# Retention attention and a feed-forward block on one core: v scaled for the states on GpSimd alone, late steps reordered

## The chip, the cores and the metric

One Trainium2 chip, one core of it. The metric is the device time of one execution in microseconds. Before the change three runs gave 206.89, 207.63 and 212.83 us, median 207.63. One execution was profiled: its own time is 207.04 us, the span from its first to its last instruction 205.2 us.

## What is computed

The reference, cut to its core. Batch 4, 8 heads, 768 positions, head width 64; then a feed-forward block with 512 and 2048 columns:

```python
gamma = 1.0 - 2.0 ** (-5.0 - np.arange(H))
for t in range(S):
    state = gamma * state + einsum('bhd,bhe->bhde', k[:, :, t], v[:, :, t])
    y[:, :, t] = scale * einsum('bhd,bhde->bhe', q[:, :, t], state)
x = y.transpose(0, 2, 1, 3).reshape(B, S, H * D)
xn = (x - mean) / np.sqrt(var + 1e-06) * g_ln
out = x + np.maximum(xn @ w_ch1, 0.0) @ w_ch2
```

All arrays come in and go out as float32; the kernel works in bfloat16 with float32 in PSUM.

## The kernel before

**Tiles.** The 4 x 768 positions are cut into 24 tiles of 128 positions: tiles 0 to 3 are the first chunk of each batch element, and tiles 4 to 23 are the later chunks, five per element. Up to tile 7 each tile has its own visit; from tile 8 on they come in pairs, (8, 9) to (22, 23).

**One tile's way.** `k`, `q`, `v` load a tile by DMA from GpSimd's queue (L361), and `gk`, `gq`, `gv` are gates behind them: a copy of one element out of the tile just loaded, on GpSimd (L390), which holds that queue until the load has landed. `tr` transposes q and k of a tile by DMA on SyncE's queue (L404). `eq` scales q (L410, VectorE). `vis` makes the scores of a pair on PE into the PSUM banks X0 to X3 (L419) and adds q times the state into Y0 and Y1 (L425). `am` multiplies the scores by the decay mask (L432, VectorE), `py` multiplies them with v (L447, PE). `bn`, `sr`, `rt` and `nb` make mean, 1/deviation and shift (L455, L586, L595, L590), `xc` copies y to SBUF (L471, ScalarE), `xg` normalizes it (L599, ScalarE), `ex` transposes that by DMA (L524).

**The state.** It is kept by chunks. `vg` makes v times the decay of each position and head (L478 on ScalarE, L481 on GpSimd), `pd` multiplies it with k and adds it up in the PSUM bank PD (L489), `pb` scales that into the bfloat16 `state` (L500 on ScalarE, L504 on VectorE). There are three buffers each for `vg` and `state`. The `vg` step in both forms:

```python
if eng == "A":
    for h in range(H):
        nc.scalar.activation(out=slot(vgs, chunk(t))[:, h, :], in_=v_of(t)[:, h, :],
                             func=AF.Copy, scale=vsc[:, c, h:h + 1])
    return
nc.gpsimd.tensor_tensor(
    out=slot(vgs, chunk(t)), in0=v_of(t),
    in1=vsc[:, c, :].unsqueeze(2).to_broadcast([P, H, D]), op=ALU.mult)
```

On ScalarE it is eight instructions, one for a head; on GpSimd it is one.

**The feed-forward block.** Tiles are put in 14 groups: eight of one tile, four of two, two of four. `m` is a first product into an X bank (L549), `r` its ReLU out of the bank into `h` (L560 on ScalarE, L562 on VectorE). For the first eight tiles `z` is the second product (L567) and `ad` adds x (L575); for these tiles the gain is in the normalized input, and `wg0` to `wg3` later multiply it into the four column blocks of the first weights (L607 on ScalarE, L609 on VectorE). The later tiles use Strassen's scheme with seven products: `s` is one product of the second multiplication (L736), `sa` the differences it needs (L725, VectorE), `o` the additions into the output tile `osb` (L750, VectorE), `tm` and `wm` the weight combinations (L619, L630). The last two groups use it for the first multiplication too: `f` products (L670), `fs` copies out of PSUM (L684, ScalarE), `fo` additions (L697, VectorE), `fq` and `fr` ReLUs (L702; L711 on ScalarE or L709 on VectorE). `st` stores a tile from ScalarE's queue.

**The order.** `ORDER`, lines 30 to 100, is a list of 1043 tokens written out. A loop at the end of the kernel emits each in turn, so each engine gets its instructions in the list's order and runs them in that order. A token's parts are the step, its tile or group, the engine after the first slash (A ScalarE, D VectorE, S SyncE's queue, nothing for the step's usual one), and the PSUM banks after the second. `vg10/A` is the state's v of tile 10 on ScalarE, `vg20/` that of tile 20 on GpSimd.

Of the kernel before, what the change touches and what calls it, by code (L numbers as in the profile page):

```python
# [52 lines left out]
am11a ad5 py10 r6_4/A py11 v14 pd11 m7_4//X1 bn11 pb12/A gq14 gk13 z6_0//M wg3/D st1/A gk15 r7_4/A
v13 pd12 bn10 m8_14//X0 sr11 xc11a q15 xc10b rt11 m8_8//X1 pb13 xc11b xc10a v15 sr10 nb11 z6_1 rt10
xg11b nb10 rs6 eq12 xg10b r8_14/A gk14 tr14 z6_2 wg1/D r8_8/A z6_3 v16 xg10a eq13 xg11a ex11/S
vis12//X0,X1,X2,X3 ad6 pd2 gv14 am13b vg14/ z7_0//M ex10/S pb14/A am12a m8_12//X3 gv13 am13a gq15
tr15 m8_2//X0 am12b tm4 py13 r8_2/A py12 z7_1 xc13a k16 xc13b bn12 r8_12/A pd14 m8_0//X0 vg15/A q16
bn13 z7_2 k17 sr13 m8_6//X1 xc12a rt13 q17 eq14 sr12 sq7 nb13 z7_3 rt12 pb15 xg13a v17 xg13b xc12b
m8_10//X2 ex13/S rs7 nb12 r8_6/A ad7 gv16 vg16/ r8_0/A m8_4//X1 r8_10/A gv15 xg12b k18 tm3 m9_8//X0
xg12a r8_4/A ex12/S pd15 st2/A eq15 s8_1//M r9_8/A sa8_1 st7/A gk17 vis14//X0,X1,X2,X3 pb16/A sa8_2  # L60
s8_5 gq17 am14a tr16 am14b pd16 gv17 m9_0//X0 gk16 am15a py14 am15b m9_4//X1 gk18 q20 py15 st3/A
m9_2//X2 tr17 bn15 r9_0/A k20 r9_4/A m9_6//X3 sa8_4 vg3/A q18 m10_2//X0 bn14 r9_6/A m9_12//X1 sa8_3
r9_2/A q19 sr14 s8_2//X3 sr15 r10_2/A o8_1 k19 xc15b vg17/A rt14 rt15 s8_6 nb15 pb17 gq20 s8_3 o8_2
r9_12/A eq16 xg15a m9_10//X0 xg15b o8_3 xc15a eq17 xc14b gq18 tr18 m9_14//X1 xc14a o8_4 v19 r9_10/A
nb14 wm3 xg14b s8_7 xg14a gq16 r9_14/A pd17 o8_5 vis16//X0,X1,X2,X3 pb18/A sa10_1 v18 tr19 s8_4
am16b gk19 am16a pd3 m10_4//X1 v20 ex15/S am17a py16 gq19 o8_6 st5/A m10_6//X0 ex14/S am17b st4/A
pb19/A bn16 s10_1//M tr20 py17 sa10_3 sr16 m10_10//X2 r10_6/A sa10_2 st6/A s10_5 rt16 r10_10/A
sa10_4 xc16b m10_12//X0 bn17 r10_4/A gv18 v21 m10_8//X1 wm1 sr17 gv19 xc17b k21 xc17a s10_2//X2
xc16a r10_8/A gk20 rt17 nb16 nb17 o10_1 m10_14//X3 r10_12/A vg20/ xg16b xg16a s10_6 xg17a q21 eq18
r10_14/A o10_2 s10_3 xg17b eq19 v22 vg19/A vis18//X0,X1,X2,X3 o10_3 o10_4 pd19 am19a s10_7 am18a  # L70
gk21 m10_0//X2 am18b q22 am19b m11_6//X0 k22 r10_0/A o10_5 pb20/A py18 sa12_1 q23 py19 s10_4 bn18
r11_6/A tr21 vg22/ pd20 m11_14//X0 o10_6 sr18 rt18 ex16/S vg21/ nb18 m11_0//X1 bn19 r11_14/A gv20
xc19b s12_1//M ex17/S gq21 eq20 r11_0/A wm2 sr19 s12_5 xg18b k23 xc18b pb21/A rt19 sa12_2 m11_8//X0
v23 nb19 sa12_3 xg19a m11_4//X1 xg18a o12_1 xg19b r11_8/A s12_2//X2 ex19/S sa12_4 xc19a r11_4/A wm4
pd21 s12_6 xc18a ex18/S pb22/A o12_2 s12_3 eq21 pd22 vis20//X0,X1,X2,X3 o12_3 tr22 o12_4 s12_7 am20a
pb23/A am21a f12_1_1//X0 am20b f12_0_1//PD m11_2//X2 xt12_1 fs12_0_1 am21b fs12_1_1 f12_0_5//X1
xt12_2 py20 tr23 o12_5 fs12_0_5 f12_0_2//X3 xt12_3 f12_0_6 r11_2/A fo12_0_1 py21 fs12_0_2 f12_0_3
bn20 f12_1_6 xc21a s12_4 st8/A fo12_0_2 fs12_1_2 f12_1_5//X2 xc21b xt12_4 xc20b f12_1_7 bn21
fs12_1_5 m11_10//X1 sr20 xc20a fo12_1_3 sr21 f12_1_3 r11_10/A rt20 rt21 m11_12//X3 nb20 nb21 eq23
xg20a eq22 f12_1_4 r11_12/A o12_6 f12_1_2//X1 fo12_1_2 xg20b f12_0_7 xg21b xg21a fo12_1_1 s14_1//M  # L80
fq12_1 ex21/S fo12_0_3 st13/A vis22//X0,X1,X2,X3 sa14_1 ex20/S f12_0_4 am23a s14_5 am23b f12_2_1//X2
am22b f12_3_1//X3 st9/A am22a py23 fs12_2_1 f12_2_5//X1 sa14_2 fs12_3_1 py22 f12_2_6 fs12_2_5 sa14_3
f12_3_6 fs12_2_2 sa14_4 f12_2_3 xc23a f12_3_5//X0 fs12_3_2 fo12_2_2 f12_2_7 fq12_0 o14_1 f12_3_7
st10/A f12_3_2//X1 xc22b bn22 fr12_0_1/A s14_6 fs12_3_5 bn23 s14_3 sr22 s14_2//PD rt22 sr23 o14_3
rt23 nb22 o14_4 f12_3_3 xg22b nb23 xg22a fo12_3_3 s14_7 xg23a ex22/S xc22a fo12_3_2 xg23b f12_3_4
xc23b o14_2 fr12_1_1/A f12_2_2//X0 o14_5 ex23/S f13_0_1//Y0 fr12_1_2/D fo12_2_1 s14_4 fo12_3_1
fs13_0_1 f13_0_2//X0 fo12_2_3 st11/A f13_2_1//X1 fq12_3 fo13_0_1 f13_1_1//Y1 fr12_2_1/A f12_2_4
# [763 lines left out]
```

## Time and profile before

| | us |
|---|---|
| median of three runs | 207.63 |
| the profiled execution | 207.04 |
| its span | 205.2 |
| PE busy | 194.9 |
| VectorE (DVE) busy | 165.0 |
| ScalarE (ACT) busy | 126.0 |
| GpSimd (POOL) busy | 94.2 |

The granted clock of the TensorE is 0.998 over the span. Busy time is time with an instruction on the engine; issues of DMAs from ScalarE and SyncE are not in it. In a row of the waits stand engine, what waited, `<-` what ended the wait, then us in total, times, and the longest. In a row of the timeline stand the start and the length in us, engine, line, operation, the tile written `<-` the tiles read, the shape and the count of instructions merged in the row; in brackets the idle time ahead of it and what ended it. A table by windows gives the window, its width, and each engine's busy time in it with the number of instructions. A row with three times and slashes has the shortest, the median and the longest instruction of a line in ns.

### The profile page before, as it was taken

Reading aid. Unit: us, or ns where it says so; the run is one execution under the profiler, and the core shown is the slowest. Engines: PE = TensorE matmul, PEld = TensorE weight load, DVE = VectorE, ACT = ScalarE, POOL = GpSimd, SP = SyncE. Lnnn points to the kernel's source line nnn. Section 1 sums busy time; section 2 is a strip of 40 time slices with the busy share of each in tenths; the row PEclk is TensorE's granted clock in tenths of the full one; section 3 lists DMA queues with packets and bytes.
Section 4 is the critical chain, followed back from the end, with each engine's and each line's share of the span. In section 5 each row is a group of like instructions: output and inputs, shape, how many; then the busy total and the mean of one; then the engine's idle time right before and its main releaser. Section 6 shows DMA issues by size and latency. Waiting matters only on the chain.

```text
span 205.2 us, 5787 instructions
## 1 busy us (share of the span) xinstructions
PE 194.9 (95%) x2292; PEld 159.3 (78%) x2303; DVE 165.0 (80%) x388; ACT 126.0 (61%) x316; POOL 94.2 (46%) x139
## 2 busy tenths in 40 slices
PE   7998999999999999998997998999999999999992
PEld 3568999897546576666986987988989888888881
DVE  6687899587258799967787996988988998879961
ACT  6376644641426998589499496895949896543000
POOL 8997593694597398695806198600000000000000
PEclk9999999999999999999999999999999999999999
DMA  8999999999999999999999999988142140102224
GB/s 128 173 182 180 159 194 167 175 181 156 159 111 166 147 118 168 169 155 209 179 133 107 205 190 104 137 75 126 56 144 65 26 131 0 51 3 102 104 82 177
DMA packets 110477, 27.16 MB, mean 132 GB/s; under 512 B 103153, under 2 KB 107505, under 8 KB 110450
## 3 DMA queue, kind: packets, MB, share of 16 engines
...
q14 instruction: 9, 0.07, 0.1%
...
## 4 chain that ended last, share of the span: by engine, by line
PE 37%; ACT 13%; DVE 3%; issue 2%; ACTq 0%; DVEq 0%
PE M L736 11%; PE X L670 8%; PE Y L736 5%; PE X L549 5%; ACT xn L599 3%; ACT vg L478 3%; ACT h L560 3%; PE Y L670 2%; PE PD L670 2%; ACT x_all L471 1%; PE X L736 1%; PE X L419 1%; PE Y L447 1%; ACT state L500 1%; PE PD L736 1%
## 5 line engine op out<-in xcount | busy, mean ns | idle before, releaser
L549 PE MATMUL X<-xnt,w 128*128 128x128 bf16 (+1 forms) x768 | 64.0, 237 | 0.9 <-ACT h L560 0.9
L549 PEld LDWEIGHTS <-w 128*128 128x128 bf16 x768 | 53.9, 98 | 6.0 <-issue 1.3
L560 ACT ACTIVATE h<-X 128x512 bf16<-128x512 f32 x57 | 33.5, 607 | 17.8 <-PE X L549 17.6
L432 DVE TENSOR_TENSOR asb<-X,mask 128x512 bf16<-128x512 f32 x48 | 30.3, 682 | 1.7 <-PE X L419 1.4
L736 PEld LDWEIGHTS <-h 128*128 128x128 bf16 x256 | 24.7, 98 | 3.3 <-issue 0.4
L567 PE MATMUL M<-w,h 128*128 128x512 bf16 x87 | 22.1, 379 | 0.5 <-issue 0.2
L567 PEld LDWEIGHTS <-h 128*128 128x128 bf16 x128 | 11.8, 98 | 11.7
L736 PEld LDWEIGHTS <-sum 128*128 128x128 bf16 x192 | 18.7, 98 | 2.6 <-issue 0.4
L455 DVE BATCH_NORM_STATS2 bns<-Y 128x6 f32<-128x256 f32 (+1 forms) x39 | 16.3, 451 | 5.2 <-PE Y L447 3.8
L471 ACT CAST x_all<-Y 128x256 bf16<-128x256 f32 (+1 forms) x39 | 14.8, 410 | 8.4 <-DVE xn L465 7.8
L361 POOL DMA_DIRECT2D v<-in_v_dram x20 | 17.8, 890 | 3.2 <-DMA w<-in_moe_w_ch_dram 2.2
L599 ACT ACTIVATE xn<-Y,shift,rstd 128x256 bf16<-128x256 f32 x32 | 16.7, 580 | 1.5 <-DVE shift L590 0.8
L361 POOL DMA_DIRECT2D qk<-in_k_dram x17 | 15.4, 906 | 1.0 <-issue 1.0
L361 POOL DMA_DIRECT2D qk<-in_q_dram x17 | 15.0, 889 | 1.1 <-issue 1.1
L500 ACT ACTIVATE state<-PD,gch 128x128 bf16<-128x128 f32 x40 | 11.7, 401 | 4.7 <-PE PD L489 3.6
L481 POOL TENSOR_TENSOR vg<-v,vsc 128x512 bf16<-128x512 bf16 x11 | 11.4, 1042 | 6.5 <-DMA v<-in_v_dram 6.5
L750 DVE TENSOR_TENSOR osb<-M,x_all 128x256 f32<-128x256 f32 (+1 forms) x18 | 9.1, 506 | 5.5 <-PE M L736 5.5
L390 POOL COPY scrap<-qk 1x1 bf16<-1x1 bf16 x28 | 8.9, 320 | 10.0 <-DMA qk<-in_q_dram 6.1
L736 PE MATMUL M<-early,sum 128*128 128x256 bf16 x96 | 12.4, 273 | 0.2 <-DVE osb L750 0.2
L736 PE MATMUL M<-w,h 128*128 128x256 bf16 x96 | 12.4, 273 | 0.0
L711 ACT ACTIVATE h<-h 128x1024 bf16<-128x1024 bf16 (+1 forms) x10 | 8.5, 862 | 5.5 <-DVE h L697 5.5
L725 DVE TENSOR_TENSOR sum<-h,sum 128x1024 bf16<-128x1024 bf16 x16 | 10.9, 681 | 0.1
...
## 6 DMA issues: line engine op xcount, KB each, us to landing
...
```

The costliest lines, as they stand in the source:

```text
L361: nc.gpsimd.dma_start(out=dst, in_=tok[kind][TILES[t]])
L432: nc.vector.tensor_tensor(out=slot(asb, t)[:, :, par, :], in0=bank(("pa", t, par)).rearrange("p (i t) -> p i t", t=P), in1=mask.rearrange( ...
L455: nc.vector.bn_stats(out=bns[:, t, i, :], in_=x)
L471: nc.scalar.copy(out=dst, in_=src)
L481: nc.gpsimd.tensor_tensor(out=slot(vgs, chunk(t)), in0=v_of(t), in1=vsc[:, c, :].unsqueeze(2).to_broadcast([P, H, D]), op=ALU.mult)
L500: nc.scalar.activation(out=slot(state, chunk(t) - 1)[:, i, :], in_=pd[:, i, :], func=AF.Copy, scale=gch[:, c - 1, i:i + 1])
L549: nc.tensor.matmul(bank(("mm", g, ho))[:, j * n * P:(j + 1) * n * P], lhsT=w1[:, ko, (ho + j) * P:(ho + j + 1) * P], rhs=x[:, x0:x0 + n, k ...
L560: nc.scalar.activation(out=dst, in_=src, func=AF.Relu)
L567: nc.tensor.matmul(bank(("m2", t)), lhsT=slot(h1, t // 4)[:, ho, t % 4 * P:(t % 4 + 1) * P], rhs=w2[:, ho, :], start=(ho == 0), stop=(ho = ...
L599: nc.scalar.activation(out=heads(slot(xns, t))[:, :, half], in_=split(y_of(t, half)), func=AF.Identity, bias=shift[:, t:t + 1], scale=rstd ...
L670: nc.tensor.matmul(f_bank(g, j, i)[:, n * w:(n + 1) * w], lhsT=f_left(i, ko)[:, (nb * j + n) * P:(nb * j + n + 1) * P], rhs=f_right(g, i)[ ...
L736: nc.tensor.matmul(product(t, i), lhsT=left(t, i)[:, ho, :], rhs=right[i][:, ho, :], start=(ho == 0 and i in (1, 2)), stop=(ho == HK - 1), ...
```

## The change

Only the table changes, from its 306th token on; no step is added or removed. The diff is 52 lines of tokens out and 53 in, so all later line numbers grow by one. Its first lines:

```diff
-z2_3 ad0 tr10 gq10 z3_0//M v12 gk11 st0/A ad2 z3_1 tr11 eq8 q13 vis8//X2,X1,X3,X0 wg0/A tm1 z3_2
-am8a am8b z3_3 am9b pd9 am9a m7_12//X1 pb10/A gv10 gv11 ad3 q12 py8 py9 vg10/A z4_0//M bn9 z4_1 bn8
+z2_3 ad0 tr10 gq10 z3_0//M v12 gk11 st0/A ad2 z3_1 tr11 eq8 q13 vis8//X2,X1,X3,X0 tm1 z3_2 am8b am9a
+pd9 z3_3 vg11/ pb10/A am8a m7_12//X1 am9b vg10/ ad3 py9 r7_12/A py8 q12 z4_0//M bn8 xc9a gv11 z4_1
...
```

What changes beside the order:

- `vg10`, `vg11`, `vg15`, `vg3`, `vg17` and `vg19` go from ScalarE to GpSimd, 48 activations for six `tensor_tensor`. These are all that ScalarE had.
- `wg2` goes from ScalarE to VectorE and `wg3` from VectorE to ScalarE, four instructions each.
- Of the late ReLUs `fr`, `fr12_1_2`, `fr12_3_2`, `fr13_1_1`, `fr13_0_1` and `fr13_2_2` go from VectorE to ScalarE, and `fr12_0_2`, `fr13_2_1` and `fr13_0_2` from ScalarE to VectorE. The ones that end in `_1` are 128x1024, the others 128x512.

Two places show how instructions moved. First ScalarE between the pairs (12, 13) and (14, 15), near the wait of PE at 93.9 us: `h10` and `h11` are ReLU outputs, `vg0` is `vg15`, `rstd` a square root, `xn` the normalized tiles. Before:

```order
L560 ACTIVATE h10_129<-X3_64 128x2x256
L478 ACTIVATE vg0_117<-v2_104,vsc_84 128x64 x8
L586 ACTIVATE rstd_91<-mv_90,epsb_76 128x1
L471 CAST x_all_96<-Y0_65 128x4x64
L586 ACTIVATE rstd_91<-mv_90,epsb_76 128x1
L537 ACTIVATE rstd_91<-mv_90,epsb_76 128x1
L599 ACTIVATE xn1_123<-Y0_65,shift_92,rstd_91 128x4x64
L599 ACTIVATE xn1_123<-Y1_66,shift_92,rstd_91 128x4x64
L471 CAST x_all_96<-Y1_66 128x4x64
L560 ACTIVATE h10_129<-X1_62 128x2x256
```

Now:

```order
L561 ACTIVATE h10_129<-X0_61 128x2x256
L472 CAST x_all_96<-Y1_66 128x4x64
L587 ACTIVATE rstd_91<-mv_90,epsb_76 128x1
L600 ACTIVATE xn0_122<-Y0_65,shift_92,rstd_91 128x4x64
L561 ACTIVATE h10_129<-X2_63 128x2x256
L600 ACTIVATE xn1_123<-Y0_65,shift_92,rstd_91 128x4x64
L561 ACTIVATE h10_129<-X1_62 128x2x256
L600 ACTIVATE xn1_123<-Y1_66,shift_92,rstd_91 128x4x64
```

The eight activations of the `vg` are gone, and the ReLUs stand between the normalizations instead of behind two of them.

Second GpSimd's queue behind the visit of pair (8, 9), where the first two of the six `vg` arrive: `vg2` is `vg11` out of `v7`, `vg1` is `vg10` out of `v6`, `scrap` rows are gates. Before:

```order
L361 DMA qk_111<-in_q_dram 128x8x64
L390 COPY scrap_71<-v6_108 1x1
L390 COPY scrap_71<-v7_109 1x1
L361 DMA qk_111<-in_q_dram 128x8x64
L390 COPY scrap_71<-qk_111 1x1
L361 DMA qk_111<-in_k_dram 128x8x64
L390 COPY scrap_71<-v8_110 1x1
```

Now:

```order
L362 DMA qk_111<-in_q_dram 128x8x64
L482 TENSOR_TENSOR vg2_119<-v7_109,vsc_84 128x512
L482 TENSOR_TENSOR vg1_118<-v6_108,vsc_84 128x512
L362 DMA qk_111<-in_q_dram 128x8x64
L391 COPY scrap_71<-v7_109 1x1
L362 DMA qk_111<-in_k_dram 128x8x64
L391 COPY scrap_71<-v8_110 1x1
L391 COPY scrap_71<-v6_108 1x1
```

Both `vg` now stand ahead of the issue of the next q, and they wait themselves for the landing of v for which a gate waited there before.

More of the change, by code (lines that the diff above doesn't have):

```diff
@@ L53 @@
[L53 to L87, printed above, removed]
@@ new lines @@
+pd9 z3_3 vg11/ pb10/A am8a m7_12//X1 am9b vg10/ ad3 py9 r7_12/A py8 q12 z4_0//M bn8 xc9a gv11 z4_1
+xc8b bn9 k13 z4_2 xc9b sr8 sr9 z4_3 rt8 rt9 nb8 nb9 eq10 xg8a m7_8//X0 xg8b ad4 xc8a ex8/S xg9b pd10
+gv12 z5_0//M gv10 xg9a pb11 gk12 q14 r7_8/A z5_1 ex9/S eq11 gq11 k15 wg2/D pd11 vis10//X0,X1,X2,X3
+tr12 pb12/A k14 z5_2 am11a sq6 v14 tr13 wg3/A am11b z5_3 rs6 vg12/ am10a py11 m7_4//X2 am10b gq13
+vg2/ ad5 py10 m6_4//X0 xc11b bn11 gq14 z6_0//M r6_4/A bn10 pd12 gk15 gk13 z6_1 gq12 v13 pb13 sr10
@@ new lines @@
+sr11 st1/A z6_2 q15 rt10 r7_4/A rt11 nb10 nb11 wg1/D xg11a z6_3 v15 xg11b xg10a m8_14//X0 ex11/S ad6
+gk14 gv14 xc10b vg14/ xc10a m8_8//X1 xc11a xg10b tr14 v16 r8_14/A eq12 pd2 z7_0//M eq13 r8_8/A tm2
+ex10/S pb14/A vis12//X0,X1,X2,X3 gv13 z7_1 wg0/A am12a am12b pd14 m8_4//X0 gq15 tr15 k16 am13a py12
+am13b m8_6//X1 k17 sq7 bn12 r8_4/A m8_12//X2 q16 tm4 sr12 r8_6/A py13 m8_2//X0 q17 xc12a r8_12/A
+rt12 bn13 m8_0//X1 vg15/ xc13a xc13b nb12 m8_10//X2 r8_2/A gv15 gv16 eq14 xc12b k18 sr13 z7_2 xg12a
@@ new lines @@
+rt13 rs7 nb13 pb15 r8_10/A v17 z7_3 xg13a vg16/ r8_0/A m9_8//X0 ad7 xg13b xg12b pd15 eq15 ex13/S
+s8_1//M sa8_1 r9_8/A pb16/A vis14//X0,X1,X2,X3 ex12/S st2/A s8_5 am14b tr16 gk18 am15a pd16 q20
+m9_0//X1 am14a gk17 m9_12//X2 gq17 am15b tr17 gv17 gk16 k20 tm3 py14 py15 m9_10//X0 q18 st3/A r9_0/A
+sa8_3 m9_6//X3 q19 r9_12/A bn15 st6/A m9_2//X1 k19 r9_6/A sa8_2 s8_2//X2 bn14 vg3/ r9_2/A xc15a
+m10_2//X3 r9_10/A sa8_4 vg17/ xc14a sr14 m9_14//X0 o8_1 sr15 xc14b gq20 r10_2/A rt14 nb14 s8_6 pb17
+xc15b r9_14/A rt15 s8_3 o8_2 gq18 nb15 eq16 xg15a m10_14//X0 xg15b o8_3 eq17 xg14b ex15/S m9_4//X1
@@ new lines @@
+v19 o8_4 r10_14/A wm3 xg14a s8_7 gq16 tr18 r9_4/A st4/A v18 pd17 vis16//X0,X1,X2,X3 o8_5 pb18/A
+sa10_1 tr19 gk19 v20 s8_4 am16b am16a pd3 m10_12//X1 am17a py16 st5/A am17b m10_4//X0 xc16b o8_6
+gv19 r10_12/A vg19/ bn16 m10_10//X2 st8/A st7/A tr20 py17 sr16 m10_6//X1 pb19/A rt16 sa10_2 ex14/S
+s10_1//M sa10_3 r10_6/A gv18 bn17 r10_4/A m10_0//X3 v21 xc17a wm1 s10_5 sr17 gq19 r10_0/A k21
+r10_10/A m10_8//X0 nb16 gk20 eq18 xg16a rt17 s10_2//X1 o10_1 xg16b q21 xc16a nb17 sa10_4 ex16/S
+xc17b s10_6 r10_8/A o10_2 v22 xg17b eq19 s10_3 xg17a sa12_1 vis18//X0,X1,X2,X3 o10_3 vg21/ o10_4
@@ new lines @@
+pd19 am19b s10_7 pb20/A vg20/ am18b m11_8//X3 am18a gk21 q22 o10_5 m11_6//X1 r11_8/A am19a q23
+sa12_3 py18 py19 pd20 m11_14//X0 bn19 tr21 gv20 pb21/A gq21 vg22/ s10_4 bn18 sr19 ex17/S k22 pd21
+m11_4//X2 rt19 o10_6 sr18 r11_6/A rt18 nb19 sa12_2 xc18b s12_1//M r11_4/A nb18 k23 wm2 xg19a s12_5
+xg19b v23 xg18a eq20 m11_0//X1 ex19/S xg18b o12_1 xc19b s12_2//X2 sa12_4 xc19a ex18/S xc18a r11_0/A
+wm4 s12_6 pb22/A s12_3 eq21 r11_14/A o12_2 pd22 o12_3 vis20//X0,X1,X2,X3 o12_4 tr22 s12_7 am20b
+pb23/A am20a f12_1_1//X1 am21a m11_2//PD fs12_1_1 xt12_1 f12_0_1//X0 am21b f12_1_5//X2 xt12_2
@@ new lines @@
+fs12_0_1 py20 o12_5 py21 fs12_1_5 m11_12//X3 xt12_3 tr23 r11_2/A bn21 f12_1_6 r11_12/A f12_0_2//PD
+bn20 fs12_1_2 f12_0_6 m11_10//X3 xc20b fo12_0_1 sr20 fs12_0_2 rt20 f12_1_7 xt12_4 sr21 xc20a nb20
+f12_0_5//PD eq22 xg20a f12_0_7 fo12_1_3 fs12_0_5 s12_4 rt21 xc21a eq23 r11_10/A nb21 fo12_0_3
+f12_1_4 xg21a f12_1_2//X3 o12_6 xg21b f12_1_3 sa14_1 xg20b f12_0_4 xc21b fo12_1_1 ex20/S f12_0_3
+fq12_1 fo12_1_2 s14_1//M fq12_0 sa14_2 st13/A ex21/S vis22//X0,X1,X2,X3 st12/A fo12_0_2 s14_5 am22b
+am23b f12_3_5//PD f12_3_1//X1 am23a f12_2_1//X3 am22a f12_2_5//X2 st9/A fs12_3_5 py23 sa14_4 py22
@@ new lines @@
+fs12_2_1 s14_2//X0 bn22 fs12_2_5 f12_2_6 fs12_3_1 bn23 f12_3_3 fs12_2_2 f12_2_3 sr22 f12_3_6 o14_1
+sr23 fr12_1_2/A f12_2_7 rt22 rt23 fs12_3_2 s14_6 nb22 fo12_2_2 xg22b fo12_2_3 f12_3_7 xc22a xc22b
+f13_1_1//X2 fo12_3_2 xc23a xg22a s14_3 o14_2 nb23 ex22/S fo12_3_3 xg23a f12_2_4 xg23b o14_3
+f13_0_2//X0 sa14_3 xc23b f13_0_1//PD ex23/S fr12_0_1/A f12_2_2//Y0 o14_4 f12_3_4 fo12_2_1 st11/A
+s14_7 fq12_3 fr12_0_2/D fs13_0_1 f12_3_2//Y0 o14_5 fr12_1_1/A f13_2_1//X1 fo12_3_1 f13_1_2//Y1
+xt13_1 s14_4 fs13_1_1 xt13_2 st14/A xt13_3 f13_0_5//Y0 fq12_2 o14_6 f13_0_6 st10/A fo13_1_1
@@ new lines @@
+f13_2_2//X3 fs13_0_5 fr12_3_1/D f13_1_5//M fs13_0_2 fo13_0_1 f13_0_3 fs13_1_5 f13_1_6 fo13_0_2
+fr12_2_1/A f13_0_7 f13_3_1//X0 fo13_0_3 fs13_2_1 f13_3_2//Y0 sa16_1 fr12_3_2/A f13_1_3 f13_3_5//Y1
+fs13_1_2 xt13_4 f13_2_6 fo13_2_1 fs13_3_1 f13_1_7 fo13_3_1 f13_2_5//X3 f13_3_6 fo13_1_3 s16_1//Y0
+fo13_1_2 fs13_3_5 sa16_3 fs13_2_5 s16_5 fr13_0_1/A sa16_2 f13_3_3 o16_1 f13_2_3 fs13_2_2 f13_1_4
+fs13_3_2 fo13_2_2 f13_2_7 fr12_2_2/A f13_3_7 fr13_1_1/A s16_6 fo13_3_3 fq13_1 fr13_2_1/D s18_1//M
+fo13_2_3 fr13_1_2/A f13_3_4 sa16_4 s16_2//X2 fq13_3 sa18_1 fr13_3_2/A s16_3 sa18_3 fr13_2_2/A sa18_2
@@ L100 @@
+f13_0_4 f13_2_4 fo13_3_2 fq13_0 s18_5 o16_3 fr13_3_1/A sa18_4 s18_2//X0 o16_4 fq13_2 o18_1 s16_7
+st15/A o16_2 s18_6 st16/A o16_5 fr13_0_2/D o18_2 s20_1//Y1 sa20_1 s16_4 sa20_2 s20_5 s22_1//PD
+sa22_1 o20_1 s18_3 o16_6 s20_6 st17/A o18_3 sa20_4 s22_5 sa22_2 s20_3 s20_2//X0 sa22_4 o18_4
+s22_2//X1 o20_3 o22_1 s18_7 o22_2 s22_6 o18_5 sa20_3 s22_3 o20_4 sa22_3 s18_4 o22_3 o20_2 s20_7
+o22_4 o18_6 st22/A s22_7 o20_5 st18/A st20/A s20_4 st19/A o22_5 st23b/A s22_4 o20_6 st21/A o22_6
+st23a/A
 """.split()
```

15 lines of the change are left out of this document (removed).

## The prediction

> **What bounds the kernel now.** I read the page first, then the waits, then the timeline around each wait of the PE, then a table by stage.
>
> ```profile
> PE 194.9 (95%) x2292; PEld 159.3 (78%) x2303; DVE 165.0 (80%) x388; ACT 126.0 (61%) x316; POOL 94.2 (46%) x139
> ```
>
> PE is busy for 95% of the span, but a busy PE is not PE at its peak, so the share alone settles nothing. What can be won is the time in which the next matmul was due and waited. The list of waits has these for PE (the larger ones against `zeros` and `trq` belong to the first 20 us, where both kernels are the same):
>
> ```profile
> PE X L419 <- ACT h L560: 1.2, 1, 1.2
> PE X L549 <- ACT h L560: 0.9, 1, 0.9
> PE PD L489 <- ACT vg L478: 0.5, 2, 0.3
> PE X L419 <- ACT h L702: 0.4, 1, 0.4
> PE M L736 <- DVE osb L750: 0.2, 1, 0.2
> PE PD L489 <- ACT state L500: 0.2, 1, 0.2
> ```
>
> Seven waits, 3.4 us. The view counts idle time, and the drawn tail of the last matmul hides some of each wait. The same eight matmuls in the timeline and in the chain of waits:
>
> ```profile
> 113.39 1.04 PE L549 MATMUL X<-xnt,w 128*128 128x256 bf16 x8
> 113.55 0.87 PE X L549 x8
> ```
>
> They hold PE for 0.87 us and are drawn 1.04 long. So each wait costs about 0.16 us more than shown, an estimate from these two rows: 3.4 + 7 x 0.16 = 4.5 us. That is all that a better order of the late part can win on PE: 207.04 - 4.5 = 202.5 us is the floor.
>
> Now who made PE wait. The table by stage, cut where the score matmuls of each pair of tiles begin:
>
> ```profile
> core 0: us, PE busy (x) PEld busy (x) DVE busy (x) ACT busy (x) POOL busy (x), PEclk, DMA share, GB/s
> 61.73:72.36 10.63, 10.52 (x119) 6.54 (x121) 8.95 (x22) 9.06 (x30) 6.32 (x12) 1.00 1.63 151
> 72.36:82.99 10.63, 10.42 (x127) 7.17 (x129) 9.87 (x29) 10.00 (x29) 9.55 (x16) 1.00 1.66 149
> 82.99:96.82 13.83, 12.70 (x139) 9.59 (x140) 11.08 (x24) 10.88 (x34) 10.25 (x18) 1.00 2.10 168
> 96.82:110.11 13.29, 13.23 (x161) 11.92 (x161) 11.19 (x28) 10.71 (x36) 7.09 (x12) 1.00 1.49 158
> 110.11:123.96 13.85, 12.42 (x149) 10.81 (x149) 11.29 (x25) 10.29 (x29) 7.52 (x14) 1.00 1.55 174
> 123.96:138.80 14.84, 14.11 (x169) 12.36 (x170) 13.11 (x30) 11.51 (x36) 7.13 (x9) 1.00 1.44 108
> 138.80:151.50 12.70, 12.35 (x151) 11.00 (x150) 11.72 (x30) 10.13 (x24) 0.00 (x0) 1.00 0.46 105
> 151.50:201.40 49.90, 49.90 (x492) 44.56 (x491) 42.68 (x91) 23.81 (x45) 0.00 (x0) 1.00 0.23 73
> ```
>
> After 151.5 PE has no hole at all, and ScalarE is half idle: nothing is to be won there. Between 61.7 and 138.8 ScalarE and VectorE are each at 74 to 94%, so any of their instructions that stands in the wrong place in line reaches PE. The timeline shows what stood there:
>
> ```profile
> 88.58 2.01 ACT L478 ACTIVATE vg<-v,vsc 128x64 bf16<-128x64 bf16 x8
> 90.59 1.03 POOL L481 TENSOR_TENSOR vg<-v,vsc 128x512 bf16<-128x512 bf16 x1
> 90.89 1.02 DVE L410 TENSOR_TENSOR trq<-tr,qsc 128x512 bf16<-128x512 bf16 x1
> 93.89 1.91 PE L549 MATMUL X<-xnt,w 128*128 128x256 bf16 x16 [0.94 <-ACT h L560]
> ...
> 105.35 2.03 ACT L478 ACTIVATE vg<-v,vsc 128x64 bf16<-128x64 bf16 x8
> 110.80 0.66 ACT L560 ACTIVATE h<-X 128x512 bf16<-128x512 f32 x1
> 111.51 0.60 PE L419 MATMUL X<-trq,tr 64*128 64x128 bf16 x15 [1.18 <-ACT h L560]
> ...
> 120.33 1.13 DVE L590 SCALAR_TENSOR_TENSOR shift<-mv,rstd 128x1 f32<-128x1 f32 x2
> 120.34 1.03 POOL L481 TENSOR_TENSOR vg<-v,vsc 128x512 bf16<-128x512 bf16 x1
> 122.12 1.03 PE L736 MATMUL M<-early,sum 128*128 128x256 bf16 x8 [0.24 <-DVE osb L750]
> 123.72 2.02 ACT L478 ACTIVATE vg<-v,vsc 128x64 bf16<-128x64 bf16 x8
> 125.31 0.22 PE L489 MATMUL PD<-vg,qk 128*128 128x128 bf16 x1 [0.25 <-ACT vg L478]
> 125.78 0.22 PE L489 MATMUL PD<-vg,qk 128*128 128x128 bf16 x1 [0.26 <-ACT vg L478]
> ```
>
> Three of the holes have a `vg` of ScalarE in their past: eight activations, 2.0 us in which nothing else passes on that engine. At 125 PE waits for the `vg` itself. At 93.9 and 111.5 it waits for a ReLU that empties a PSUM bank and that stood behind other ScalarE work which a `vg` had pushed back (the one at 88.58 for the first, the one at 105.35 for the second, whose ReLU started at 110.80 only).
>
> **The change, part by part.** *1. Six `vg` go from ScalarE to GpSimd.*
>
> ```profile
> 61.73:151.50 89.77, 5.79 (x56) 12.08 (x48) 7.22 (x7) 1.00 1.47 144
> L481 POOL TENSOR_TENSOR vg<-v,vsc 128x512 bf16<-128x512 bf16 x11 | 11.4, 1042 | 6.5 <-DMA v<-in_v_dram 6.5
> ```
>
> The first row is the `vg` tiles' own work on PE, ScalarE and GpSimd: 48 activations, all that there are, take 12.08 us of ScalarE, and all 48 go. In the six stages from 61.73 to 138.80 ScalarE is busy 62.5 of 77.1 us, 81%; without these 12.1 it is 50.4, 65%. The three holes with a `vg` behind them are 0.94 + 1.18 + 0.25 + 0.26 = 2.63 us of idle, and with 0.16 for each of the four waits 3.3 us. I count all of it as **-3.3**: an ACT queue shorter by 2 us ahead of a ReLU that came 0.9 or 1.2 us late covers the lateness.
>
> On GpSimd six take 6 x 1.042 = 6.25 us. From 61.73 to 123.96 that engine is busy 6.32 + 9.55 + 10.25 + 7.09 + 7.52 = 40.7 of 62.2 us, and what it waits for is landings of v above all:
>
> ```profile
> POOL scrap L390 <- DMA v<-in_v_dram: 13.7, 6, 5.6
> POOL vg L481 <- DMA v<-in_v_dram: 6.5, 4, 5.0
> ```
>
> So 6.25 us fit into 21.5 us of idle time. Behind each new `vg` in that queue stand the issues of k, q and v; the first two new ones come after q13 was issued and ahead of q12, 2.1 us, and the gates behind them would have waited for landings anyway. Cost on PE: **0** so long as these waits are the cover; without it the issues come up to 6.25 us late and the scores of a pair with them.
>
> *2. A GpSimd `vg` can hold VectorE.* In the fence above a `trq` took 1.02 us beside a GpSimd `vg`, and a one-column `shift` took 1.07, each until that `vg` was done. The rows of these lines and of a third, a `sum` beside the `vg` at 127.78:
>
> ```profile
> L410 DVE TENSOR_TENSOR trq<-tr,qsc x17: 370/415/1017, 44.2 to 148.3; 128x512 bf16<-128x512 bf16 x17
> L590 DVE SCALAR_TENSOR_TENSOR shift<-mv,rstd x16: 139/153/1067, 68.7 to 161.2; 128x1 f32<-128x1 f32 x16
> L725 DVE TENSOR_TENSOR sum<-h x8: 681/684/951, 96.2 to 190.5; 128x1024 bf16<-128x1024 bf16 x8
> ```
>
> Held: 1.017 - 0.415 + 1.067 - 0.153 + 0.951 - 0.684 = 1.78 us over the seven `vg` that GpSimd does in this part, 0.25 each. Six more bring 1.5 us of VectorE time. Of the 1.78, PE felt 0.40 for certain (the hole at 122.1, 0.24 + 0.16, whose `osb` stood behind the held `shift`) and at most 0.60 more (the held `trq` is ahead of the ReLU of 93.9): between a quarter and a bit over a half. Bounds: 0 if no new one meets such an instruction, and 6 x 0.91 = 5.5 us if each meets one as badly as the `shift` was met and PE feels all of it. I take half of 1.5, **+0.8**, the upper end of what PE felt so far, because the freed ScalarE no longer covers VectorE's lateness.
> The Trainium skill says in "SBUF — State Buffer", section "Who interferes with whom", that a VectorE instruction with two SBUF inputs contends with a GpSimd instruction that reads SBUF, and that whichever comes second waits for the other's whole instruction. This trace agrees: `trq`, `shift` and `sum` have two such inputs, and the `shift` took 1.067 instead of 0.153 us. It is the rule that speaks against the change, and taken alone it is the third rival below.
>
> *3. `wg2` goes from ScalarE to VectorE, `wg3` the other way.* Equal pieces: **0** in the sum of either engine. A `wg` on ScalarE is four activations of 0.71 us in a row, so it can now stand ahead of a ReLU after 72 us; the stage there loses a `vg` of 2.0 us on ScalarE by point 1.
>
> *4. Late ReLUs (`fr`) change engines, five to ScalarE and three to VectorE.* They lie after 151.5, where PE has no hole, ScalarE is busy 23.8 of 49.9 us, and VectorE gets less: **0**; uncovered it would be one more ReLU of 128x1024 on ScalarE in front of PE, 1.08 us by its group in the profile.
>
> *5. Some 740 late steps stand in another order.* The trace of before can't price this. Below nothing: the three small holes that no `vg` explains (122.1, the wait for `state`, the wait for the ReLU of L702) are 0.24 + 0.2 + 0.4 idle and may go, 1.3 us with the tails. Above: an order planned so tightly leaves new places where a ReLU has barely time; the two worst of before cost 1.1 and 1.3 us, so 2.4. I take **+0.5**, one more hole of the size of the one by L702.
>
> Sum: -3.3 + 0 + 0.8 + 0 + 0 + 0.5 = -2.0 on the profiled execution's 207.04 us, whose span is 205.2: **205.0 us**. The median of the three runs, 207.63, is 0.6 above that execution; against it 205.0 is 1.3% less. About 2%, 4 us, is what a measurement of this kernel tells from no change.
>
> **The rivals.**
> *The holes only move (22%).* ScalarE is emptied, but VectorE's load stays at 80 to 93% of each stage, and a ReLU or an `am` of the new order is late elsewhere. For it: two of the large holes have a VectorE step in their past. Against it: ScalarE names itself in six of the seven waits. The -3.3 is then given back by half to all: 206.2 to 207.8, say 207.0.
> *Nearly all holes go (11%).* The floor is 202.5; with one hole of 0.5 us left, 203.0. For it: ScalarE has a third of its time free then. Against it: the holds of VectorE stay.
> *VectorE becomes the bound through the held instructions (12%): slower.* Place: the `nb`, `eq` and `sa` steps beside the six new `vg`, behind which the `xg`, the score matmuls and the Strassen products stand. Price: up to 6 x 0.91 = 5.5 us, against -3.3: 207.04 + 2.2 = 209.2. It decides from 3.3 us of such holds on the path, four bad meetings in six. For it: one `shift` did it before. Against it: of seven `vg` three met one, 0.25 us each in the mean.
> That the change does not do what it says is excluded by the order: no `vg` is left on ScalarE.
>
> **How the numbers follow.** Forecast 55%, 204.0 to 206.2 by itself (points 2 and 5 between 0.3 and 2.5 us). Adding the rivals' times until under 2 in 10 is left out gives 203.3 to 208.2. Faster than 203.5 (2% under 207.63) is the better half of the second rival and a little of the forecast: 0.07. Slower than 211.8 needs more than the third rival's full price: 0.03. Within 2%: 0.90.
>
> **What would show it.** Right: no ScalarE `vg` rows, ScalarE's busy time down by about 10 us, GpSimd's up by 6; the waits of PE for `h` of L560 and for `vg` at under 1 us together; the score matmuls of the last pair some 2 us before 151.5; after them the same 50 us. Point 2 right: more `shift`, `trq` or `sum` rows of around 1 us, each beside a GpSimd `vg`. Wrong: PE waiting for `tr` or for DMA (GpSimd's queue was late), holes after the last pair's scores (points 4 and 5), or waits for `h` as long as before though ScalarE is idle ahead of them.

## The result and the profile after

| | before | after |
|---|---|---|
| median of 20 runs of each, us | 207.81 | 206.19 |
| ratio to before, 95% interval | 1 | 0.991, 0.988 to 0.994 |
| the profiled execution, us | 207.04 | 204.79 |
| its span, us | 205.2 | 203.0 |

Some executions of a kernel are slower as a whole; the ratios leave these out on both sides, so they are not quotients of the medians. The same kernel, measured again, gave 0.988 [0.983, 0.992] (the first experiment): about 1% faster, less than the 2% that the prediction counted as surely told from no change, and close to the -2.0 us of the forecast. The share of each engine, and the chain that ended last:

```profile
PE 195.3 (96%) x2303; PEld 159.3 (78%) x2303; DVE 167.1 (82%) x386; ACT 117.0 (58%) x270; POOL 98.9 (49%) x145
...
PE 45%; DMA 4%; ACT 2%; DVE 1%; ACTq 0%; issue 0%
```

ScalarE lost 9.0 us, GpSimd gained 4.7 and VectorE 2.1. In the chain of before ScalarE had 13%; now it has 2%, and DMA comes in with 4%. The waits of the kernel after, those of PE from the late part and the two large ones of GpSimd:

```profile
PE X L550 <- DMA xnt<-xn: 1.3, 1, 1.3
PE M L737 <- ACT xn L600: 0.3, 1, 0.3
...
POOL scrap L391 <- DMA v<-in_v_dram: 11.0, 4, 4.2
POOL vg L482 <- DMA v<-in_v_dram: 10.1, 4, 4.9
```

No wait for a ReLU (`h` of L561) and none for `vg` is left; one wait for a transposed `xn` is new. What stood there, from the timeline:

```profile
109.95 8.61 SPq L405 DMA_TRANSPOSE tr<-qk  x3
118.66 3.25 SPq L525 DMA_TRANSPOSE xnt<-xn  x2
124.80 2.04 POOL L482 TENSOR_TENSOR vg<-v,vsc 128x512 bf16<-128x512 bf16 x2 [3.51 <-DMA v<-in_v_dram]
126.19 1.92 PE L550 MATMUL X<-xnt,w 128*128 128x256 bf16 x16 [1.35 <-DMA xnt<-xn]
...
149.77 0.62 PE L420 MATMUL X<-trq,tr 64*128 64x128 bf16 x16
```

The SyncE queue issues in the list's order. The new order puts `ex14` (the transposition of tile 14's `xn`) behind `tr18`, `tr19` and `tr20`. Their three issues take 8.61 us, so `ex14` leaves at 118.66; its data land at 126.14, and PE waits for them until 126.19. The last pair's scores begin at 149.77 instead of 151.50.

One sum puts all runs on one scale. From the starts of the matmuls in the trace I take every gap after 60 us that is over 0.12 us longer than the median step behind matmuls of that line and shape, and add up the excess. Six gaps of before, 0.21 to 0.33 us each and 1.4 together, are left out: in each stands a weight load of L567 whose matmul has no record, so PE was not idle there. The page of before counts 2292 matmuls to 2303 weight loads, that of after 2303 to 2303.

| profiled execution | holes of PE, us | span, us | span less holes |
|---|---|---|---|
| before | 5.1 | 205.2 | 200.1 |
| after | 2.8 | 203.0 | 200.2 |
| after, another execution | 5.4 | 205.6 | 200.2 |
| only the six `vg` moved | 8.7 | 208.3 | 199.6 |
| only the order changed | 9.7 | 210.1 | 200.4 |

The last column stays within 1 us while the span varies by 7: the holes are the time. From before to after the holes lose 2.3 us and the span 2.2.

### The profile page after: what moved, and what is told of

Same layout as the page of the kernel before. It is cut to its first block, busy times and chain, and to the rows that moved or that the text cites. A ratio compares the mean times of both kernels' runs of the same rounds, so it can differ in the third digit from the quotient of the medians.

```text
span 203.0 us, 5754 instructions
## 1 busy us (share of the span) xinstructions
PE 195.3 (96%) x2303; PEld 159.3 (78%) x2303; DVE 167.1 (82%) x386; ACT 117.0 (58%) x270; POOL 98.9 (49%) x145
## 4 chain that ended last, share of the span: by engine, by line
PE 45%; DMA 4%; ACT 2%; DVE 1%; ACTq 0%; issue 0%
PE M L737 11%; PE X L671 8%; PE X L550 7%; PE Y L737 5%; DMA xnt<-xn 4%; PE X L737 3%; PE PD L737 3%; PE PD L671 2%; PE Y L671 2%; PE X L420 1%; PE Y L448 1%; ACT xn L600 1%; ACT h L561 1%; PE PD L490 1%; PE Y L426 0%; PE M L671 0%
## 5 line engine op out<-in xcount | busy, mean ns | idle before, releaser
L550 PE MATMUL X<-xnt,w 128*128 128x128 bf16 (+1 forms) x760 | 62.9, 237 | 1.3 <-DMA xnt<-xn 1.3
L550 PEld LDWEIGHTS <-w 128*128 128x128 bf16 x768 | 53.8, 98 | 6.1 <-DMA xnt<-xn 1.6
L561 ACT ACTIVATE h<-X 128x512 bf16<-128x512 f32 x56 | 33.3, 608 | 17.9 <-PE X L550 17.7
L568 PE MATMUL M<-w,h 128*128 128x512 bf16 x96 | 23.0, 379 | 0.0
L482 POOL TENSOR_TENSOR vg<-v,vsc 128x512 bf16<-128x512 bf16 x16 | 16.7, 1047 | 10.1 <-DMA v<-in_v_dram 10.1
L391 POOL COPY scrap<-qk 1x1 bf16<-1x1 bf16 x28 | 8.1, 289 | 6.6 <-DMA qk<-in_k_dram 3.7
L737 PE MATMUL M<-w,h 128*128 128x256 bf16 x80 | 10.4, 272 | 0.4 <-ACT xn L600 0.3
L737 PE MATMUL M<-early,sum 128*128 128x256 bf16 x80 | 10.4, 273 | 0.0
L757 PE MATMUL PD<-zeros 128*128 128x512 bf16 (+1 forms) x33 | 9.2, 417 | 1.2 <-DVE zeros L271 1.2
L671 PEld LDWEIGHTS <-w 128*128 128x128 bf16 x96 | 9.4, 98 | 1.1
```

What stands on the lines that cost most here:

```text
L482: nc.gpsimd.tensor_tensor(out=slot(vgs, chunk(t)), in0=v_of(t), in1=vsc[:, c, :].unsqueeze(2).to_broadcast([P, H, D]), op=ALU.mult)
L550: nc.tensor.matmul(bank(("mm", g, ho))[:, j * n * P:(j + 1) * n * P], lhsT=w1[:, ko, (ho + j) * P:(ho + j + 1) * P], rhs=x[:, x0:x0 + n, k ...
L561: nc.scalar.activation(out=dst, in_=src, func=AF.Relu)
L568: nc.tensor.matmul(bank(("m2", t)), lhsT=slot(h1, t // 4)[:, ho, t % 4 * P:(t % 4 + 1) * P], rhs=w2[:, ho, :], start=(ho == 0), stop=(ho = ...
L671: nc.tensor.matmul(f_bank(g, j, i)[:, n * w:(n + 1) * w], lhsT=f_left(i, ko)[:, (nb * j + n) * P:(nb * j + n + 1) * P], rhs=f_right(g, i)[ ...
L737: nc.tensor.matmul(product(t, i), lhsT=left(t, i)[:, ho, :], rhs=right[i][:, ho, :], start=(ho == 0 and i in (1, 2)), stop=(ho == HK - 1), ...
```

## The experiments

A token of the table is quoted with its neighbours where the place matters. "Its own before" is the kernel before, run beside each on the same chip.

### The changed kernel again

Unaltered, to see what one execution of it varies by.

> The changed kernel once more, unaltered, as the yardstick for the three others. Every theory: ratio to the kernel before about 0.991, as measured (0.988 to 0.994). Theory of a missed transpose: PE again waits 1 us or more for the transposed xn of the pair (14, 15), about 125 us into the span. Rival, that this wait was an accident of the one profiled execution: no such wait, or one at another transpose.

Measured: 205.28 us, its own before 207.96, ratio 0.988 [0.983, 0.992]. The execution that was profiled was one of the longer ones, 207.44 us with a span of 205.6, and the comparison with the 204.79 one is of use. Its timeline:

```profile
119.27 1.14 DVE L591 SCALAR_TENSOR_TENSOR shift<-mv,rstd 128x1 f32<-128x1 f32 x1
119.36 1.03 POOL L482 TENSOR_TENSOR vg<-v,vsc 128x512 bf16<-128x512 bf16 x1
120.74 0.67 DVE L751 TENSOR_TENSOR osb<-M,x_all 128x512 f32<-128x512 f32 x1
121.46 0.71 PE L737 MATMUL M<-early,sum 128*128 128x256 bf16 x5 [1.15 <-DVE osb L751]
...
128.39 2.04 POOL L482 TENSOR_TENSOR vg<-v,vsc 128x512 bf16<-128x512 bf16 x2 [0.71 <-DMA v<-in_v_dram]
130.48 0.39 PE L490 MATMUL PD<-vg,qk 128*128 128x128 bf16 x4 [1.41 <-POOL vg L482]
```

In this execution `vg` of GpSimd and `shift` of VectorE meet at 119.3: the `shift` takes 1.14 us, the `osb` behind it is late, and PE waits 1.15. At 128.4 two `vg` in a row wait for one landing, and PE waits 1.41 for the second. Neither hole is in the other execution; the one at `xnt` is in both (1.5 us each). The gate ahead of the `vg` at 119.36 had waited 5.3 us for v. So where GpSimd meets VectorE is not fixed by the order alone: it depends on when v lands.

### Only the six `vg`

The order of before, with `vg10`, `vg11`, `vg15`, `vg3`, `vg17` and `vg19` on GpSimd:

```diff
-am8a am8b z3_3 am9b pd9 am9a m7_12//X1 pb10/A gv10 gv11 ad3 q12 py8 py9 vg10/A z4_0//M bn9 z4_1 bn8
+am8a am8b z3_3 am9b pd9 am9a m7_12//X1 pb10/A gv10 gv11 ad3 q12 py8 py9 vg10/ z4_0//M bn9 z4_1 bn8
...
```

> The order of before, with nothing changed but the engine of the six vg (GpSimd in place of ScalarE). Theory A, ScalarE's 2 us blocks were the cause: the waits of PE at 93.9, 111.5 and 125 us go or shrink to under a third, ratio about 0.985 to 0.99, nearly all of the change's gain. Rival B, the order is the cause: the blocks only free ScalarE for work that isn't ready, ratio 0.995 to 1.005. Rival C, GpSimd is late: placed where ScalarE had them, the vg wait in GpSimd's queue for landings of v and hold back the loads behind them, or VectorE is held; ratio over 1.005, PE waits for PD's vg or for tr.

Measured: 210.24 us, ratio 1.010 [1.007, 1.014]: slower than before. The rows that tell why:

```profile
92.08 1.14 DVE L590 SCALAR_TENSOR_TENSOR shift<-mv,rstd 128x1 f32<-128x1 f32 x1
92.17 1.03 POOL L481 TENSOR_TENSOR vg<-v,vsc 128x512 bf16<-128x512 bf16 x1
93.30 1.02 ACT L599 ACTIVATE xn<-Y,shift,rstd 128x256 bf16<-128x256 f32 x2 [1.03 <-issue]
94.47 1.10 ACT L560 ACTIVATE h<-X 128x512 bf16<-128x512 f32 x2
...
122.65 2.43 DVE L410 TENSOR_TENSOR trq<-tr,qsc 128x512 bf16<-128x512 bf16 x1
123.39 1.03 POOL L481 TENSOR_TENSOR vg<-v,vsc 128x512 bf16<-128x512 bf16 x1
124.38 0.94 POOL L361 DMA_DIRECT2D qk<-in_q_dram  x1
125.31 0.88 POOL L361 DMA_DIRECT2D v<-in_v_dram  x1
126.20 1.06 POOL L481 TENSOR_TENSOR vg<-v,vsc 128x512 bf16<-128x512 bf16 x1
127.32 0.38 PE L489 MATMUL PD<-vg,qk 128*128 128x128 bf16 x4 [1.55 <-POOL vg L481]
...
130.11 2.62 DVE L725 TENSOR_TENSOR sum<-h 128x1024 bf16<-128x1024 bf16 x1 [1.08 <-ACT h L560]
```

The hole at 93 is still there, and the list of waits still puts it down to the ReLU, 1.5 us. Yet ScalarE no longer does a `vg` there: its `xn` waits for the held `shift`, and the ReLU stands behind that `xn`. Already ahead of this a weight combination on VectorE, `early`, took 2.64 us from 86.88 on, beside a moved `vg` and DMA issues of GpSimd, against 1.21 in before, and the statistics behind it were late. At the third place, 111.5 us in before, 0.4 us is left of the hole. At 125 the wait for a `vg` remains too, on another engine, since this one stands behind two issues of GpSimd. The holds add up to 7.0 us over thirteen `vg` (every VectorE instruction beside a `vg` less the median of its kind over all profiled executions, a shared one counted once); in the kernel before it was 1.8 over seven. The move alone exchanges one late engine for another.

### Only the order

The order of after, the six `vg` back on ScalarE (`vg11/` to `vg11/A` and so on). The swaps of `wg` and `fr` stay in.

> The order of after, with the six vg given back to ScalarE, eight activations each. Theory A: the 12 us of ScalarE come back as waits of PE for ReLUs and for vg, 3 us or more in sum, ratio 0.997 to 1.01. Rival B, the order is the cause: the ratio stays at 0.988 to 0.994 since the new order has ScalarE's steps in better places.

Measured: 210.90 us, ratio 1.010 [1.005, 1.015]: slower than before as well. Its waits:

```profile
PE X L550 <- ACT h L561: 2.4, 2, 1.3
PE X L550 <- DMA xnt<-xn: 1.8, 1, 1.8
PE M L737 <- DVE osb L751: 1.3, 1, 1.3
PE M L568 <- DVE osb L576: 1.2, 1, 1.2
```

The order of after was laid for a ScalarE without `vg`. With it the ReLUs are late again (2.4 us), the `osb` too. Each half costs 1.0%, both together gain about 1.0%. So neither the move nor the reordering (with the swaps) has a value of its own here, and the gain is in that the order fits the engines. What the swaps would do in the old order was not run.

### Tile 14's transposition ahead of three others

```diff
-v19 o8_4 r10_14/A wm3 xg14a s8_7 gq16 tr18 r9_4/A st4/A v18 pd17 vis16//X0,X1,X2,X3 o8_5 pb18/A
+v19 o8_4 r10_14/A wm3 xg14a ex14/S s8_7 gq16 tr18 r9_4/A st4/A v18 pd17 vis16//X0,X1,X2,X3 o8_5 pb18/A
...
-gv19 r10_12/A vg19/ bn16 m10_10//X2 st8/A st7/A tr20 py17 sr16 m10_6//X1 pb19/A rt16 sa10_2 ex14/S
+gv19 r10_12/A vg19/ bn16 m10_10//X2 st8/A st7/A tr20 py17 sr16 m10_6//X1 pb19/A rt16 sa10_2
```

> The changed kernel with one step moved: the DMA transpose of xn of tile 14 is issued right after that tile is normalized, ahead of the transposes of q and k of tiles 18, 19 and 20 instead of behind them. Theory of a missed transpose: the wait of PE for xnt at 125 us (1.35 idle) goes, the profiled span drops by about 1.5 us to 201.5, ratio to before 0.981 to 0.986. Rival, the transposes of q and k are then late in its place: PE or VectorE waits for tr before the scores of the pair (18, 19), ratio 0.989 or more.

Measured: 206.23 us, ratio 0.982 [0.976, 0.988]; lowest run 203.34. The profiled execution has a span of 205.5 us and not the expected 201.5. Its waits have no `xnt` any more, but two of PE for `vg`:

```profile
PE PD L490 <- POOL vg L482: 1.9, 2, 1.3
```

That the hole is gone would not show its cause by itself: in the profile of the `shift` with one tensor input, below, `ex14` has its late place and PE has no wait for `xnt` either. The landings show it. Issued in its late place, `ex14` landed at 126.14 and 126.64 us in the two executions of the changed kernel, about 1.5 us after PE was due to use it; in the profile named it landed at 124.83, and PE came to it at 126.29. Issued at 111.05 here, it had landed by 117.1, nine microseconds ahead of its use at 126.75. So in the late place it lands within 2 us of its use, on one side or the other, and PE waits in some executions only; in the early place it is not what PE waits for, in three profiles of three. The same kernel measured once more:

> The kernel with tile 14's transpose issued early once more (first time 0.982, 0.976 to 0.988, with scattered runs), to settle whether it beats the changed kernel (0.9909 over 20 runs, 0.9876 beside it). Theory of the missed transpose: ratio 0.979 to 0.986, no wait of PE for xnt near 125 us. Rival, the hole is only handed on to the vg of tile 20 behind it: ratio 0.986 to 0.992 and a wait for vg of 1.3 us or more.

Measured: 206.43 us, ratio 0.984 [0.977, 0.990], lowest 202.74. Both ratios are below the changed kernel's 0.991 and 0.988 by their centre, but the intervals touch, and the medians over all runs divide to 0.992 both times (206.23 / 207.96, 206.43 / 208.16), as they do for the changed kernel (206.19 / 207.81). A gain over the changed kernel is not shown. Its best executions are the fastest of the study. The execution profiled the second time, 211.54 us, again has no wait for `xnt` near 125 us, but one of 2.3 us at 111 for a transposition that stands further ahead in the queue, and PE waits 2.1 us in two waits for `asb` near 78 us, behind three pieces of `wg2` of 1.1 to 1.3 us on VectorE.

### `vg20` ahead of `vg21` as well

On top of the last, `vg20/` moved to just before `vg21/`, so that it need not wait for the later landing.

> The changed kernel with tile 14's transpose issued early as in the fourth run, and vg of tile 20 ahead of that of tile 21 in GpSimd's queue (v of tile 20 is loaded first and its product with k is wanted first). Theory: the wait of PE for vg at 128.9 us (1.4 idle in two of three profiles) goes as well, ratio 0.975 to 0.983, profiled execution under 204 us. Rival, v of tile 21 was not what vg of tile 20 waited for, or the engine's queue gets late elsewhere: the wait for vg remains, ratio 0.983 to 0.99.

Measured: 206.52 us, ratio 0.988 [0.981, 0.994], which misses what was expected. The wait for `vg` is gone and another has its place:

```profile
PE PD L490 <- DMA qk<-in_k_dram: 2.5, 1, 2.5
```

PE's `pd` then waits for k of a late tile at 137.5 us. I can't say from this run whether the moved `vg` made that load late or its landing varied by itself.

### A `shift` with one tensor input

The `nb` step of the changed kernel in another form, same arithmetic:

```diff
-        nc.vector.scalar_tensor_tensor(out=shift[:, t:t + 1], in0=mv[:, t, 0:1], scalar=-1.0,
-                                       in1=rstd[:, t:t + 1], op0=ALU.mult, op1=ALU.mult)
+        nc.vector.tensor_scalar(out=shift[:, t:t + 1], in0=mv[:, t, 0:1], scalar1=rstd[:, t:t + 1],
+                                scalar2=-1.0, op0=ALU.mult, op1=ALU.mult)
```

> The changed kernel with the shift (nb) written as a product of one tensor and two scalars, so that it has one tensor input in SBUF in place of two. Theory, GpSimd's vg holds a VectorE instruction through its second tensor input: no shift row over 0.3 us is left (before: one or two of 0.7 to 1.1 us in each profile), trq and sum rows of about 1 us stay possible, the ratio to the kernel before is 0.98 to 0.99, equal to or better than the changed kernel's 0.988 to 0.991. Rival, any VectorE instruction that starts beside a vg can be held, or shift is late for another reason: shift rows of 0.7 us or more remain, ratio 0.988 to 0.994.

Measured: 206.48 us, ratio 0.987 [0.980, 0.993]. All 16 (shortest, median, longest in ns):

```profile
L591 DVE TENSOR_SCALAR shift<-mv,rstd x16: 159/206/215, 68.8 to 160.4; 128x1 f32<-128x1 f32 x16
```

None was held, where the `shift` of before had reached 1067 ns. Only two of the 16 met a `vg`, but they did so where the changed kernel's had met one in its other execution: 0.21 us here against 1.14, and 0.19 against 0.67. The first of the two, with the instruction behind it:

```profile
120.41 0.21 DVE L591 TENSOR_SCALAR shift<-mv,rstd 128x1 f32<-128x1 f32 x1
120.50 1.03 POOL L482 TENSOR_TENSOR vg<-v,vsc 128x512 bf16<-128x512 bf16 x1
120.53 1.28 DVE L411 TENSOR_TENSOR trq<-tr,qsc 128x512 bf16<-128x512 bf16 x1
```

The same `vg` that leaves the `shift` alone holds the `trq`, which has two tensor inputs. That shows what the hold of the `shift` depends on: the second tensor input. The time is not clearly better; `trq` and `sum` still have two inputs, and a wait for `vg` was there, 1.3 us. The same edit on the kernel with only the six `vg` moved:

> The order of before with the six vg on GpSimd (ratio 1.010 as measured) and the shift with one tensor input. Theory that the holds of VectorE made that kernel slow: the shift held at 92 us for 0.98 us goes, and the wait of PE for the ReLU after it (1.67 us) shrinks to under 0.8; ratio 1.002 to 1.007. Rival, GpSimd's in-order queue alone made it slow (its vg for tile 19 came 1.7 us late for PE): ratio unchanged, 1.008 to 1.014.

Measured: 209.25 us, ratio 1.009 [1.004, 1.013], against 1.010 without it. The ratio is that of the rival, a late GpSimd queue. The hole at 93 us, put down to the `shift`, is gone in its profile, and the `shift` there took 0.21 us beside a `vg`. But PE waits 6.4 us for `vg` in two waits in this execution of 213.77 us, and had already lost 3.1 us ahead of that place, against 1.2 without the edit. So how the 1% splits between held VectorE instructions and a late GpSimd queue stays open.

### The swaps undone

The changed kernel with `wg2`, `wg3` and the eight `fr` back on their engines of before, the order kept.

> The changed kernel with wg2, wg3 and the eight late ReLUs (fr) given back to the engines that they had before, order kept. Theory of the prediction's points 3 and 4, that these cost and bring nothing: ratio 0.987 to 0.994 like the changed kernel. Rival, the planner needed them in its new order: PE waits for h of a late ReLU after 150 us or for the weights of wg, ratio 0.996 or more.

Measured: 211.81 us, its own before 209.24, ratio 1.007 [1.001, 1.012]. The forecast had given both swaps 0. They were taken apart, first `wg` alone:

```diff
-gv12 z5_0//M gv10 xg9a pb11 gk12 q14 r7_8/A z5_1 ex9/S eq11 gq11 k15 wg2/D pd11 vis10//X0,X1,X2,X3
-tr12 pb12/A k14 z5_2 am11a sq6 v14 tr13 wg3/A am11b z5_3 rs6 vg12/ am10a py11 m7_4//X2 am10b gq13
+gv12 z5_0//M gv10 xg9a pb11 gk12 q14 r7_8/A z5_1 ex9/S eq11 gq11 k15 wg2/A pd11 vis10//X0,X1,X2,X3
+tr12 pb12/A k14 z5_2 am11a sq6 v14 tr13 wg3/D am11b z5_3 rs6 vg12/ am10a py11 m7_4//X2 am10b gq13
```

> The changed kernel with only wg2 given back to ScalarE and wg3 to VectorE; the late ReLUs stay. Theory, wg3 on VectorE lies beside GpSimd's vg of tiles 12 and 2 in the new order and is held by them: PE waits 2 us or more for asb near 76 us, wg rows of VectorE over 1 us instead of 0.4, ratio 1.000 to 1.010, most of the loss of the run that undid both swaps (1.0065). Rival, the ReLUs made that loss: ratio 0.985 to 0.994.

Measured: 212.22 us, ratio 1.010 [1.006, 1.014]. The `wg` swap alone is worth 2% in the new order. The timeline of the profiled execution, 213.26 us, with the four pieces of `wg3` in the third row:

```profile
73.17 0.69 DVE L433 TENSOR_TENSOR asb<-X,mask 128x512 bf16<-128x512 f32 x1 [1.19 <-PE X L420]
73.65 1.82 POOL L362 DMA_DIRECT2D qk<-in_k_dram  x2
73.77 3.80 DVE L610 TENSOR_SCALAR w<-w,gcol 128x512 bf16<-128x512 bf16 x4
75.45 0.89 POOL L362 DMA_DIRECT2D v<-in_v_dram  x1
76.34 1.07 POOL L482 TENSOR_TENSOR vg<-v,vsc 128x512 bf16<-128x512 bf16 x1
77.49 0.68 DVE L433 TENSOR_TENSOR asb<-X,mask 128x512 bf16<-128x512 f32 x1
78.23 0.43 PE L448 MATMUL Y<-v,asb 128*128 128x64 bf16 x7 [3.00 <-DVE asb L433]
```

On VectorE `wg3` stands ahead of the second `am`, beside three DMA issues and a `vg` of GpSimd; its four pieces take 3.80 us where four take about 1.4 undisturbed, and PE waits 3.00 us for the `am`. In the profile with both swaps undone PE has the same wait, 3.9 us. Is it the `vg`, or only the place of `wg3`? The same kernel with `vg12` and `vg2` on ScalarE:

> As the run with wg2 and wg3 given back, and the vg of tiles 12 and 2 on ScalarE, so that GpSimd computes nothing beside wg3. Theory that the vg hold wg3: the four wg3 rows of VectorE are back at about 0.4 us each, and the wait of PE for asb near 76 us is under 0.5 us; the ratio stays near 1 because 4 us are added to ScalarE. Rival, wg3 is simply in front of the am on VectorE, or GpSimd's DMA issues hold it: the wait for asb stays at 2 us or more.

Measured: 207.21 us, ratio 0.996 [0.991, 1.001].

```profile
73.65 1.92 DVE L610 TENSOR_SCALAR w<-w,gcol 128x512 bf16<-128x512 bf16 x4
...
76.22 0.38 PE L448 MATMUL Y<-v,asb 128*128 128x64 bf16 x7 [1.12 <-DVE asb L433]
```

Without the two `vg` the pieces take 1.92 us and PE waits 1.12, more than the 0.5 expected and less than the rival's 2. So 1.9 of the 3.0 us went with the `vg`. The rest is that `wg3` stands there at all and is longer beside GpSimd's DMA issues: one piece took 0.79 us here, and one 1.12 in the run before, with issues alone beside them. The last of this group has only the eight `fr` back:

> The changed kernel with only the eight late ReLUs given back to the engines that they had before; wg2 and wg3 stay swapped. Theory (the prediction's point 4): PE has no new hole after 150 us and the ratio is that of the changed kernel, 0.985 to 0.993. Rival, these ReLUs are the part of the swaps that mattered: ratio 0.997 or more, PE or VectorE waits for them after 150 us.

Measured: 207.47 us, its own before 208.16; there is no ratio with an interval, so its time decides nothing. Its trace shows more: after 140.7 us PE has no hole at all, as in the changed kernel, and its waits of the late part are at 107.9 and 127.0 us, for an `osb` and for `vg` (2.5 us), ahead of any `fr`.

## Why the prediction was right, and where it was not

The total was right: -2.0 us on the profiled execution forecast, -2.25 measured there, and the ratio of 0.991 is -1.9 us on 207. The working behind it holds in part only, and that the total came so near is in part luck.

*1. Six `vg` to GpSimd, -3.3.* The holes behind the matmuls at 92.67, 110.11, 124.84 and 125.31 us (1.11, 1.37, 0.41 and 0.42 by the starts of the matmuls, 3.3 together) are gone, and there is no ScalarE `vg`. But the step that gave the credit to the `vg` was wrong. Moved alone they leave holes of 1.7 us each at two of the three places, because the ReLU can be late through held VectorE instructions as well as through a `vg` ahead of it, and a `vg` can be late on GpSimd too. It takes the new order as well. The cover on GpSimd, priced at 0, held in the profiled execution of the changed kernel: its waits for landings of v are 11.0 and 10.1 us, against 13.7 and 6.5. It did not in the other execution, where PE waited 1.4 us for a `vg`, nor in the old order, where it waited 1.6 us for one behind two issues. GpSimd rose by 4.7 us and not by 6: the six `vg` are 5.3 of it (16.7 less 11.4 in the groups), and its other work came out 0.6 less.

*2. Holds of VectorE, +0.8.* The mechanism is shown, by the `shift` that is never held with one input and by `wg3` with and without a `vg` beside it. The size by count of `vg`, 0.25 us each, was no law. Thirteen `vg` brought 2.4 us in one execution of the changed kernel, 3.5 in another, 7.0 in the old order. The prediction had also left out that VectorE instructions are longer beside GpSimd's DMA issues without any `vg`: by the same count 0.2 us together in before and 1.9 in the profiled execution of the changed kernel. The bound on a single meeting, 0.91, was too low: `trq` and `sum` were each held for over 1.9 us. I find no hole of PE behind one in the profiled execution, and 1.15 us of waiting in the other, so +0.8 lies between them. The rival with VectorE bound by holds, put at 209.2 us, is near what the move alone becomes (210.24), where a late GpSimd queue adds to the holds; with the new order the time does not go there.

*3. The `wg` swap, 0.* Wrong as a price: 2% in this order. I had counted equal pieces on either engine, and not that VectorE's are held beside GpSimd's work, while the eight pieces on ScalarE took 0.72 to 0.81 us in the changed kernel. The swap takes `wg3` out of the way of `vg12`. It puts `wg2` on VectorE, and that can meet a `vg` in its turn, as in the 211.54 us execution above.

*4. The `fr` swap, 0.* The trace agrees; the time alone could not have told it.

*5. The new order, +0.5.* The small holes behind the matmuls at 121.6, 138.0 and 150.9 us went (1.3 by their starts), and two more, 0.27 and 0.22. New ones came: 1.5 for `xnt` and 1.3 in six small ones, 2.8 together. That is +1.0, inside the bounds of -1.3 to 2.4. The kind was missed: I had looked for a late ReLU, and it was a transposition late in SyncE's queue. The forecast had named PE waiting for a DMA as a sign against it, with GpSimd's queue as the cause; the sign came, from another queue.

By the holes: -3.3 and +1.0 make -2.3, against the -2.2 us of the span. The two sizes that were off (2 at 0 instead of +0.8, and 5 at +1.0 instead of +0.5) made up for each other in large part. In the other execution of the changed kernel the holes were 5.4 us, and its 207.44 us are no gain over the 207.04 of before: one pair of executions could have spoken against the forecast as well.
